# Keeping V of head 0 inside the buffer that the zero fills read, and filling two regions early

## The chip, the cores and the metric

The kernel runs on one core of a Trainium2 chip. The metric is the device time of one execution in microseconds; the kernel before takes 792.94 us (median of three runs, 792.92 to 793.36). Engines are named as the profile names them: PE (matmuls), PEld (its weight loads), DVE, ACT, POOL, and SP, which here only issues transfers and waits. All transfers run on 16 DMA engines, which take work from queues: q1 is filled by SP, q10 by ACT, q0 by POOL.

## What is computed

One decode step of a transformer layer, forward and backward: a layer norm, attention of 16 query heads over 8 cached heads of K and V, a gated feed-forward block, and the gradients of all of it but the second input. Cut to what matters for the transfers:

```python
W = min(4096, max(256, Sk // 4))                  # 4096 of Sk = 32768 rows are attended
k = jnp.repeat(k_cache[:, :, Sk - W:, :], rep, axis=1)
v = jnp.repeat(v_cache[:, :, Sk - W:, :], rep, axis=1)
p = _softmax(jnp.einsum("bhqd,bhkd->bhqk", q, k) * (Dh ** -0.5), axis=-1)
o = jnp.einsum("bhqk,bhkd->bhqd", p, v)
...
_out, _vjp = jax.vjp(_f, A_x, A_k_cache, A_v_cache, A_wq, A_wo, B_w_gate, B_w_up, B_w_down)
```

The gradients of the two caches are outputs of 8 x 32768 x 256 bf16 each (134 MB). Rows 0 to 28671 of every head took no part in the attention, so their gradient is zero: 16 regions (8 heads, K and V) of 14336 KB that are only zeros. The last 4096 rows of every head are the computed gradient, 2048 KB for each of K and V. Of the inputs, 2048 KB of K and of V are read for each head, and the weights.

## The kernel before

**On-chip memory.** A tile `zeros` (128 partitions x 8192 bf16, 16 KB a partition) is cleared at the start, half on DVE (L55) and half on POOL (L56). All else that is large lives in one tile, `arena`, cut by hand into slots of 16 KB a partition: six for V (`VB`, `HELD = 6`), two at `MB`, three and some at `RB`. A slot holds K or V of one head, 32 rows of 256 on each partition.

**Phase 1** (L360 to L371) runs over heads 0 to 7. For head g, `scores` (L300) transposes K on PE, takes dot products and the softmax; `moments` (L333) scales K by the probabilities on DVE (L341), multiplies it with V on PE (L345) and accumulates the weighted sums of V and K (L349). While head g is in `moments`, `scores` of g+1 runs beside it. K and V of the next heads are loaded into slots that come free (`NEXT`, L355), from ACT's queue.

**Phase 2** (L386 to L525) is one row through the output projection, the feed-forward block and back, and waits mostly for weights and short dependent steps.

**Phase 3** (L620 to L690) runs over the heads again, in the order 2 to 7, 0, 1. For each head `dots` (L278) is run on V, the gradient of K and V is made on PE (L659) and cast into two `stage` slots by ACT and DVE (L663 to L667), and ACT's queue writes the two slots out (L669). V of heads 2 to 7 is still in its slots. V of heads 0 and 1 was overwritten in phase 1 by K of heads 3 and 4, and is loaded a second time (`V_again`, L631). Beside it POOL makes the weight gradients as outer products (L551, L580 to L583) and sends them out on its own queue. Slots of V that are done with serve as stages and hold `dg_bc` and the second copy of the first weight (`wq2A`).

**The fills.** SP's instruction stream is in order: the weight, then K and V of the first heads, then from L250 the 16 zero fills, each one transfer that writes a region of 14336 KB as 896 rows of 16 KB out of 32 of the partitions of `zeros`. Two are under way at a time (`DEEP = 2`): a fill is issued when the one two places before it has landed. Region 8 is split (`UNEVEN`, L240 to L246) into two entries of this list: a small one of 2048 KB, which is three transfers (1536, 480 and 32 KB), two of them with an outer dimension of only 3 and 2, and the remaining 12288 KB.

The Python order is not the order on an engine: a scheduler sorts each engine's instructions by its own estimates, and slots are guarded by semaphores that it derives. Only the fills and their waits are kept out of that, in program order.

Of the kernel before, what the change touches and what calls it, by code (L numbers as in the profile page):

```python
# [7 lines left out]
bf16 = mybir.dt.bfloat16  # L8
f32 = mybir.dt.float32
AX = mybir.AxisListType.X  # L10
ALU = mybir.AluOpType
# [4 lines left out]
G = 8  # L16
Dh = 256
W = 4096
T = 32
F = 1792  # L20
FH = F // 2
NB = 7
Sk = 32768
EPS = 1e-5
SCALE = 1.0 / 16.0
ZW = 8192
NZ = (Sk - W) * Dh // (128 * ZW)
ZM = 5120
DEEP = 2
UNEVEN = 8  # L30
HELD = 6
KB = 512


@with_exitstack
def kernel(
        ctx, tc, A_x, A_k_cache, A_v_cache, A_wq, A_wo, B_x, B_w_gate, B_w_up, B_w_down, grad_out,
           out_0, out_1, out_2, out_3, out_4, out_5, out_6, out_7, out_8):
    nc = tc.nc
    LD = nc.scalar  # L40
    ZQ = nc.sync

    const = ctx.enter_context(tc.tile_pool(name="const", bufs=1))
    small = ctx.enter_context(tc.tile_pool(name="small", bufs=2))
# [3 lines left out]


    VB = 0  # L50
    MB = VB + HELD * 16 * KB
    RB = MB + 32 * KB
    TOTAL = RB + 105 * KB // 2
    zeros = const.tile([128, ZW], bf16)
    nc.vector.memset(zeros[:, 0:ZM], 0.0)  # L55
    nc.gpsimd.memset(zeros[:, ZM:ZW], 0.0)  # L56
    arena = const.tile([128, TOTAL], bf16)

    def ar(off, n):
        return arena[:, off:off + n]  # L60

    def kv(off):
        return ar(off, T * Dh).rearrange("p (t d) -> p t d", d=Dh)

    V_of = [kv(VB + 16 * KB * (g % HELD)) for g in range(G)]
    K_of = [kv(o * KB) for o in (RB // KB, RB // KB + 16, MB // KB + 16, 0, 16, RB // KB, RB // KB + 16, RB // KB)]
    M_sb = [ar(MB + 4 * KB * g, 4 * KB).bitcast(f32).rearrange("p (v h d) -> p v h d", v=2, h=2) for g in range(G)]
    wqA = ar(MB, 24 * KB).rearrange("p (c j) -> p c j", c=3)
    wqB = ar(MB + 24 * KB, 4 * KB)
# [21 lines left out]
    h_row = ar(XB + FH + D, 2 * D)[0:1].bitcast(f32)  # L91
    h2_bf = ar(XB + FH, D)[0:1]

    stage = [kv(o) for o in (RB, RB + 16 * KB, VB + 32 * KB, VB + 48 * KB)]
    P3 = RB + 32 * KB
    rTm = [ar(P3 + 2 * i * KB, 2 * KB).rearrange("p (l c) -> p l c", l=8) for i in range(2)]
    R_sb = [ar(P3 + (4 + i) * KB, KB) for i in range(2)]
# [3 lines left out]
    VT_slot = [ar(P3 + 17 * KB // 2 + 2 * i * KB, 2 * KB) for i in range(3)]  # L101
    rows2 = ar(P3 + 29 * KB // 2, 2 * KB)[0:16].bitcast(f32)
    dqrow = [ar(P3 + 33 * KB // 2 + 2 * i * KB, 2 * KB)[0:16].bitcast(f32) for i in range(2)]
    dg_bc = ar(VB + 64 * KB, 2 * F).rearrange("p (i f) -> p i f", i=2)
    dq_bc = ar(MB, H * Dh)
    wst = [ar(MB + (8 + 12 * i) * KB, 12 * KB) for i in range(2)]
    wq2A = ar(VB + 72 * KB, 24 * KB).rearrange("p (c j) -> p c j", c=3)
    wq2B = ar(P3 + 33 * KB // 2, 4 * KB)

    x_bf = const.tile([1, D], bf16)  # L110
# [3 lines left out]
    wq_A = A_wq[0:384, :].rearrange("(p c) j -> p c j", c=3)  # L114
    wq_B = A_wq[384:D, :].rearrange("r (h j) -> (r h) j", h=2)
# [5 lines left out]
    ident_f = const.tile([128, 128], f32)  # L121
# [17 lines left out]
    nc.vector.reduce_sum(out=tl32, in_=ident_f[:].rearrange("p (k i) -> p k i", i=4), axis=AX)  # L139
    tl_f = const.tile([128, 8], f32)  # L140
    nc.vector.reduce_sum(out=tl_f[:], in_=tl32.rearrange("p (q l) -> p l q", q=4), axis=AX)
    half_f = const.tile([128, 4], f32)
    nc.vector.memset(half_f[:, 0:3], 1.0)
    nc.vector.memset(half_f[:, 3:4], 0.5)
# [53 lines left out]
    def load_kv(dst, cache, g, queue=LD):  # L198
        queue.dma_start(out=dst, in_=cache[0, g, Sk - W:, :].rearrange("(p t) d -> p t d", t=T))

    load_kv(K_of[0], A_k_cache, 0, ZQ)
    load_kv(V_of[0], A_v_cache, 0, ZQ)
    load_kv(K_of[1], A_k_cache, 1, ZQ)
    load_kv(V_of[1], A_v_cache, 1, ZQ)
    load_kv(V_of[2], A_v_cache, 2, ZQ)

    rstd1, xnT_f, X1_b = layernorm(x_bf[:], bf16, "ln1")
    d2_ps = ps_t.tile([128, 4], f32, tag="tmp")
# [19 lines left out]
    qT_bf = const.tile([128, 32], bf16)  # L228
    nc.vector.tensor_copy(out=qT_bf[:].rearrange("p (g k e) -> p k e g", k=2, e=2), in_=qT_ps[:])

    load_kv(K_of[2], A_k_cache, 2, ZQ)
    for g in range(3, HELD):
        load_kv(V_of[g], A_v_cache, g, ZQ)

    fills = []
    for g in range(G):
        for o in (out_2, out_3):
            reg = o[0, g, 0:Sk - W, :].rearrange("s d -> (s d)")
            n = NZ
            if len(fills) == UNEVEN:  # L240
                odd = reg[0:128 * ZW].rearrange("(r f) -> r f", f=ZW)
                n = NZ - 1
                reg = reg[128 * ZW:NZ * 128 * ZW]
                fills.append([(odd[0:96].rearrange("r f -> (r f)").rearrange("(p f) -> p f", p=128), zeros[:, 0:ZW * 3 // 4]),
                              (odd[96:126].rearrange("(e n) f -> e n f", e=3), zeros[0:12:4].unsqueeze(1).to_broadcast([3, 10, ZW])),
                              (odd[126:128], zeros[0:8:4])])  # L246
            fills.append([(reg.rearrange("(p n f) -> p n f", p=32, f=ZW), zeros[0:128:4].unsqueeze(1).to_broadcast([32, 4 * n, ZW]))])
    zsem = [tc.alloc_semaphore(f"zsem{j}") for j in range(DEEP)]
    due = [0] * DEEP
    for i, parts in enumerate(fills):  # L250
        j = i % DEEP
        if i >= DEEP:
            tc.keep_in_program_order(ZQ.wait_ge(zsem[j], due[j]))
        for dst, src in parts:
            fill = ZQ.dma_start(out=dst, in_=src)
            tc.info.no_tile_sem_insts.add(fill.ins.name)
            tc.add_to_no_dep_group("fills", fill.ins)
            tc.keep_in_program_order(fill.then_inc(zsem[j], 16))
            due[j] += 16
    for j in range(DEEP):  # L260
        filled = tc.keep_in_program_order(ZQ.wait_ge(zsem[j], due[j]))
    tc.declare_fence(filled.ins, group="fills")

    pT_all = const.tile([128, G, T, 2], bf16)
    oT_f = const.tile([128, 2, H], f32)
# [29 lines left out]
    with tc.tile_pool(name="ps_m", bufs=1, space=bass.MemoryType.PSUM) as ps_m, \  # L295
# [56 lines left out]
            for vh in range(2):  # L352
                nc.scalar.copy(out=M_sb[g][:, vh].rearrange("p h d -> p (h d)"), in_=M_ps[:, vh, :])

        NEXT = {0: ((0, 3), (0, 5)), 1: ((0, 4), (0, 6)), 3: ((1, 6),), 4: ((1, 7),), 5: ((0, 7),)}  # L355
        wo_v = A_wo.rearrange("(p j) n -> p j n", j=32)
        wd_v = B_w_down.rearrange("(h p b) n -> h p b n", h=2, b=NB)
        JW = 19
# [2 lines left out]
        for g in range(G):  # L361
            p_f = p_next
            if g + 1 < G:
                p_next = scores(g + 1)
            moments(g, p_f)
            for w, h in NEXT.get(g, ()):
                load_kv((K_of, V_of)[w][h], (A_k_cache, A_v_cache)[w], h)
            if g == G - 2:
                LD.dma_start(out=wo_sb[:, JW:], in_=wo_v[:, JW:])
                LD.dma_start(out=wd_sb, in_=wd_v[0])  # L370
# [15 lines left out]
    with tc.tile_pool(name="ps_mid", bufs=3, space=bass.MemoryType.PSUM) as ps_mid, \  # L386
# [38 lines left out]
        for h in range(2):  # L425
# [3 lines left out]
            for c in range(2):  # L429
                cs = slice(c * D, (c + 1) * D)  # L430
                for i in range(2):
                    r = 2 * c + i
# [46 lines left out]
        for jc in range(32):  # L479
# [3 lines left out]
                                in1=m8_f[:].unsqueeze(2).to_broadcast([128, 8, 32]), op=ALU.mult)  # L483
# [43 lines left out]
    with tc.tile_pool(name="work2", bufs=2) as work2, tc.tile_pool(name="lnw", bufs=1) as lnw, \  # L527
# [86 lines left out]
        plan = [[dq_all], [job_d(0), job_d(1)], [job_o(0, 13), job_o(13, 13)], [job_o(26, 6), spread_all, job_g(0)], [job_g(1), job_gB()],  # L614
                [job_q(0), job_q(1)], [job_q(2), job_qB()], []]

        order = list(range(2, G)) + [0, 1]
        V_again = [kv(VB), kv(VB + 16 * KB)]
        stc = 0
        for it, g in enumerate(order):  # L620
            V_sb = V_of[g] if it < HELD else V_again[g]
            fill_vpad(it % 2, doT_bf[:, :, 2 * g:2 * g + 2])

            def evac(q, XT, ps):
# [2 lines left out]
                else:  # L627
                    nc.vector.tensor_copy(out=XT, in_=ps)
            dpT_ps = dots(V_sb, VT_slot, vpad[it % 2], rows2, ps_t, "tmp", evac)
            if it in (4, 5):  # L630
                load_kv(V_again[it - 4], A_v_cache, it - 4)  # L631
            if it == 3:
                for c in range(3):
                    LD.dma_start(out=wq2A[:, c, :], in_=wq_A[:, c, :])
                LD.dma_start(out=wq2B, in_=wq_B)

            pds = work2.tile([128, 4, 8, 4], bf16, tag="pds")
            pv = pT_all[:, g].rearrange("p (q l) h -> p q l h", q=4)
# [10 lines left out]
            R_ps = ps_t.tile([128, 2, 2, 128], f32, tag="tmp")  # L649
            nc.tensor.matmul(R_ps[:].rearrange("p w e n -> p (w e n)"), lhsT=se, rhs=Zrow, start=True, stop=True)  # L650
            nc.scalar.copy(out=Rs.rearrange("p (w n e) -> p w e n", w=2, e=2), in_=R_ps[:])
            stV, stK = stage[stc % 4], stage[(stc + 1) % 4]
            stc += 2
            for l in range(8):
                for qp in range(2):
# [11 lines left out]
                        nc.vector.tensor_copy(out=stK[:, t:t + 2, :], in_=d_ps[:, :, 1, :])  # L667
            for o_ap, st_ in ((out_3, stV), (out_2, stK)):
                LD.dma_start(out=o_ap[0, g, Sk - W:, :].rearrange("(p t) d -> p t d", t=T), in_=st_)  # L669
            for job in plan[it]:  # L670
                job()
            if it == HELD:
                dn1 = lnw.tile([128, 5], f32)
                for c in range(3):
                    nc.vector.tensor_tensor_reduce(out=wq2A[:, c, :], in0=wq2A[:, c, :], in1=dq_bc, scale=1.0, scalar=0.0,
                                                   op0=ALU.mult, op1=ALU.add, accum_out=dn1[:, c:c + 1])
                for h in range(2):
                    nc.vector.tensor_tensor_reduce(out=wq2A[:, h, 0:HJ], in0=wq2B, in1=dq_bc[:, h * HJ:(h + 1) * HJ], scale=1.0, scalar=0.0,
                                                   op0=ALU.mult, op1=ALU.add, accum_out=dn1[:, 3 + h:4 + h])
                dcat1 = lnw.tile([128, 8], f32)  # L680
                close(dn1, dcat1)
                dxT = layernorm_bwd(dcat1, xnT_f, rstd1, dhT[:], "ln1")
                dx_ps = ps_t.tile([1, D], f32, tag="tmp")
                for c in range(3):
                    nc.tensor.matmul(dx_ps[0:1, c * 128:(c + 1) * 128], lhsT=dxT[:, c:c + 1], rhs=ident_f[:], start=True, stop=True)
                nc.tensor.matmul(dx_ps[0:1, 384:D], lhsT=dxT[:, 3:4], rhs=pair_f[:], start=True, stop=True)
                dx_bf = x_bf
                nc.vector.tensor_copy(out=dx_bf[:, 0:384].rearrange("o (p c) -> o p c", c=3), in_=dx_ps[0:1, 0:384].rearrange("o (c p) -> o p c", c=3))
                nc.vector.tensor_copy(out=dx_bf[:, 384:D], in_=dx_ps[0:1, 384:D])
                LD.dma_start(out=out_1.rearrange("a b d -> (a b) d"), in_=dx_bf[:])  # L690
# [29 lines left out]
```

## Time and profile before

| | |
|---|---|
| median of three runs | 792.94 us (792.92 to 793.36) |
| the profiled execution | 794.59 us, of which the span from first to last instruction is 792.8 us |
| DMA | 334.58 MB in 24109 packets, mean 422 GB/s; 53.58 MB read from HBM, 280.59 MB written |
| busy in the span | PE 60%, DVE 45%, ACT 25%, PEld 25%, POOL 22% |
| fills on SP's queue | 15 of 14336 KB (median 87.6 us from issue to landing), 12288, 1536, 480 and 32 KB |
| V loads | 6 from SP's queue (median 28.3 us to landing), 4 from ACT's (16.9 us), 2048 KB each |
| last instruction on POOL | issue of the last weight gradient, 732.41 us |

Times in the trace are microseconds from the start of the span. A stretch's row in the windows view has the busy time of each engine, then the granted share of the PE clock, then the share of the 16 DMA engines that was busy, and the GB/s that they moved.

### The profile page before, as it was taken

How to read it: one execution, taken by the hardware profiler on the slowest of the kernel's cores; microseconds unless marked ns; L12 is line 12 of the kernel's file. 1: busy time of each engine (PE TensorE's matmuls, PEld its weight loads, DVE VectorE, ACT ScalarE, POOL GpSimd, SP SyncE). 2: the span in 40 equal slices, each digit the busy share in tenths (PEclk: the TensorE clock that was granted, in tenths of full speed). 3: DMA queues.
4: the chain of work that ended last, by engine and by line, in shares of the span. 5: the costliest groups of instructions: out<-in, count | busy, mean ns of one | idle time of the engine just before them, and what ended most of it. 6: DMA issues, size and time to landing. Idle time of an engine off the chain costs nothing.

```text
span 792.8 us, 6367 instructions
## 1 busy us (share of the span) xinstructions
PE 476.8 (60%) x2165; PEld 201.4 (25%) x2184; DVE 358.5 (45%) x1083; ACT 198.2 (25%) x309; POOL 176.2 (22%) x93
## 2 busy tenths in 40 slices
PE   4899999999969935222325898618478273430000
PEld 1444444444424422000112433203123121000000
DVE  4266263736533631043785732965585184540000
ACT  0621325241304000010101633424244153440000
POOL 1000000000000000000000029869051865658000
PEclk9889999999998976555555999657578575555555
DMA  9999999999999999999899999999999999999997
GB/s 378 427 420 433 425 429 431 429 427 428 430 426 432 425 428 430 430 429 431 381 427 433 422 424 418 430 425 425 430 416 430 426 428 432 427 424 428 427 428 308
DMA packets 24109, 334.58 MB, mean 422 GB/s; under 512 B 1289, under 2 KB 2317, under 8 KB 3693
## 3 DMA queue, kind: packets, MB, share of 16 engines
q1 hardware_dynamic: 16229, 257.43, 76.5%
q10 hardware_dynamic: 5560, 60.23, 17.9%
q0 software_dynamic: 2288, 16.52, 5.0%
q8 instruction: 17, 0.28, 0.1%
q14 instruction: 15, 0.12, 0.0%
HBM read 53.58 MB, written 280.59 MB: 421 GB/s over the span
## 4 chain that ended last, share of the span: by engine, by line
PE 37%; DMA 20%; POOL 17%; DVE 8%; issue 6%; another core or an unknown queue 2%; ACT 1%; POOLq 0%; SPq 0%; ACTq 0%; DVEq 0%
POOL arena L551 14%; DMA out_dram<-arena 11%; PE M_ps L345 11%; PE rows_ps L288 6%; PE ok_ps L349 6%; PE tr_ps L285 6%; DVE arena L480 2%; DMA arena<-in_A_wo_dram 2%; DVE arena L341 2%; DMA arena<-in_A_k_cache_dram 2%; DMA arena<-in_B_w_down_dram 2%; DMA arena<-in_B_w_up_dram 2%; DVE arena L423 2%; DMA arena<-in_A_wq_dram 1%
## 5 line engine op out<-in xcount | busy, mean ns | idle before, releaser
L341 DVE TENSOR_SCALAR arena<-arena,p_f 128x256 bf16<-128x256 bf16 x512 | 109.0, 280 | 56.7 <-PE M_ps L345 28.0
L345 PE MATMUL M_ps<-arena 128*128 128x512 bf16 x493 | 118.9, 382 | 0.6
L285 PE MATMUL tr_ps<-ident_f,arena 128*128 128x128 f32 x512 | 96.5, 318 | 35.9 <-DMA arena<-in_A_v_cache_dram 15.6
L288 PE MATMUL rows_ps<-arena,vpad 128*16 128x512 bf16 x256 | 89.5, 445 | 8.5 <-ACT arena L626 3.1
L659 PE MATMUL d_ps<-arena 32*128 32x512 bf16 x256 | 48.6, 507 | 75.4 <-DVE arena L667 65.5
L302 ACT COPY arena<-tr_ps 128x1024 bf16<-128x1024 bf16 x64 | 63.7, 1013 | 119.6 <-PE tr_ps L285 117.8
L285 PEld LDWEIGHTS tr_ps<-ident_f,arena 128*128 128x128 f32 x512 | 63.2, 158 | 88.9 <-issue 33.7
L551 POOL TENSOR_SCALAR arena<-arena,xT 128x1792 bf16<-128x1792 bf16 (+1 forms) x9 | 60.5, 6734 | 61.2 <-DMA out_dram<-arena 33.8
L663 ACT CAST arena<-d_ps 128x512 bf16<-128x512 f32 x64 | 38.0, 593 | 103.2 <-PE d_ps L659 94.9
L373 POOL DMA_DIRECT2D arena<-in_A_wo_dram x1 | 0.7, 687 | 278.6 <-PE ok_ps L349 278.6
L345 PEld LDWEIGHTS <-arena 128*128 128x128 bf16 x512 | 48.1, 99 | 56.0 <-issue 7.7
L666 DVE CAST arena<-d_ps 128x512 bf16<-128x512 f32 x64 | 44.0, 687 | 40.4 <-PE d_ps L659 40.1
L551 POOL TENSOR_SCALAR arena<-dh_bc,oX_f 128x448 bf16<-128x448 bf16 x32 | 52.9, 1665 | 9.9 <-DMA out_dram<-arena 9.7
L349 PE MATMUL ok_ps<-arena 128*32 128x512 bf16 x256 | 52.5, 381 | 1.4 <-DVE arena L329 0.9
L667 DVE CAST arena<-d_ps 128x512 bf16<-128x512 f32 x64 | 43.5, 679 | 14.5 <-DMA out_dram<-arena 14.5
L626 ACT COPY arena<-tr_ps 128x1024 bf16<-128x1024 bf16 x32 | 32.7, 1026 | 64.8 <-PE rows_ps L288 36.5
L664 ACT CAST arena<-d_ps 128x512 bf16<-128x512 f32 x64 | 38.4, 600 | 13.5 <-DMA out_dram<-arena 13.5
L659 PEld LDWEIGHTS <-arena 32*128 32x128 bf16 x256 | 10.9, 95 | 110.1 <-DVE arena L667 72.2
L434 PE MATMUL r_ps<-arena,X2pad 128*4 128x448 bf16 x24 | 10.4, 571 | 38.8 <-DMA arena<-in_B_w_up_dram 23.7
L288 PEld LDWEIGHTS <-vpad 128*16 128x16 bf16 x256 | 17.0, 91 | 46.8 <-issue 42.0
L551 POOL TENSOR_SCALAR arena<-dh_bc,hh_f 128x448 bf16<-128x448 bf16 x14 | 19.4, 1398 | 42.8 <-PE dqb_ps L533 42.8
L384 ACT CAST arena<-bc_ps 128x448 bf16<-128x448 f32 x16 | 8.7, 541 | 80.8 <-PE bc_ps L383 69.7
(218 smaller groups left out, 429.4 us busy)
## 6 DMA issues: line engine op xcount, KB each, us to landing
out_dram<-zeros SPq DMA_DIRECT2D x15, 14336.0 KB, 87.6
out_dram<-arena ACTq DMA_DIRECT2D x16, 2048.0 KB, 29.0
arena<-in_A_v_cache_dram SPq DMA_DIRECT2D x6, 2048.0 KB, 28.3
out_dram<-zeros SPq DMA_DIRECT2D x1, 12288.0 KB, 33.7
arena<-in_A_k_cache_dram ACTq DMA_DIRECT2D x5, 2048.0 KB, 14.8
arena<-in_A_v_cache_dram ACTq DMA_DIRECT2D x4, 2048.0 KB, 16.9
arena<-in_A_k_cache_dram SPq DMA_DIRECT2D x3, 2048.0 KB, 21.0
arena<-in_A_wq_dram SPq DMA_DIRECT2D x1, 3072.0 KB, 10.1
```

The costliest lines, as they stand in the source:

```text
L285: nc.tensor.transpose(tr_ps[:, i, :], X_sb[:, 4 * q + i, :].bitcast(f32), ident_f[:])
L288: nc.tensor.matmul(rows_ps[:], lhsT=pad[:, e, 16 * q:16 * q + 16], rhs=XT.rearrange("p (n e) -> p n e", e=2)[:, :, e], start=(q == 0 and e ...
L302: sT_ps = dots(K_of[g], KT_slot, vpad[g % 2], rows1, ps_c, "cols", lambda q, XT, ps: nc.scalar.copy(out=XT, in_=ps))
L341: nc.vector.tensor_scalar(out=pK[:, i, hh, :], in0=K_sb[:, t, :], scalar1=p_f[:, 8 * i + c, hh:hh + 1], scalar2=None, op0=ALU.mult)
L345: nc.tensor.matmul(M_ps[:, vh, :], lhsT=V_sb[:, t, vh * 128:(vh + 1) * 128], rhs=pK[:, i, :, :].rearrange("p h d -> p (h d)"), start=(t == ...
L349: nc.tensor.matmul(ok_ps[32 * k:32 * (k + 1), :], lhsT=ppad[g % 2][:, t:t + 2, :].rearrange("p t h -> p (t h)"), rhs=X_sb[:, t:t + 2, :].r ...
L551: nc.gpsimd.tensor_scalar(out=buf[:, off:off + n], in0=src, scalar1=col, scalar2=None, op0=ALU.mult)
L659: nc.tensor.matmul(d_ps[:, qi].rearrange("p w d -> p (w d)"), lhsT=rm[32 * q:32 * (q + 1), l, :], rhs=Rs[32 * q:32 * (q + 1), :], start=Tr ...
L663: nc.scalar.copy(out=stV[:, t:t + 2, :], in_=d_ps[:, :, 0, :])
L664: nc.scalar.copy(out=stK[:, t:t + 2, :], in_=d_ps[:, :, 1, :])
L666: nc.vector.tensor_copy(out=stV[:, t:t + 2, :], in_=d_ps[:, :, 0, :])
L667: nc.vector.tensor_copy(out=stK[:, t:t + 2, :], in_=d_ps[:, :, 1, :])
```

## The change

The tile `zeros` is gone, and V gets a seventh slot. V of head 0 stays in slot `S[0]` for the whole kernel. Once head 0 is through `moments`, `clear_rows` (DVE) clears every fourth partition of that slot, 32 of the 128, by an AND of 32-bit words with a mask of -1 or 0 per partition. The fills from region 2 on read these 32 partitions; the other 96 keep V.

Regions 0 and 1 are filled before that, from slots 5 and 6, which POOL clears at the start (128 x 16384). These two early fills write 448 rows of 32 KB each. V of heads 5 and 6 is loaded into the slots from POOL's queue behind a wait for the early fills.

In phase 3 the order of the heads is 3, 1, 4, 5, 0, 6, 2, 7. After head 3 its slot takes a copy of slot 0 (DVE), and a load of 32 partitions puts the missing quarter of V of head 0 into that copy. V of head 2, whose slot was taken by K of head 6 and V of head 7, is loaded again into the same slot after head 0. V of head 1 is now kept. The split region 8 is one entry of the list: its four transfers are issued together on one semaphore. Stages, `dg_bc` and `wq2A` move to other slots, and `wq2A` is loaded in two parts.

```diff
+ZE = 32 * KB
+ZW = 16 * KB
+EARLY = 2
-    zeros = const.tile([128, ZW], bf16)
-    nc.vector.memset(zeros[:, 0:ZM], 0.0)
-    nc.gpsimd.memset(zeros[:, ZM:ZW], 0.0)
...
-    K_of = [kv(o * KB) for o in (RB // KB, RB // KB + 16, MB // KB + 16, 0, 16, RB // KB, RB // KB + 16, RB // KB)]
+    S = [VB + 16 * KB * i for i in range(7)]
+    V_of = [kv(S[i]) for i in (0, 1, 2, 3, 4, 5, 6, 2)]
+    K_of = [kv(o) for o in (RB, RB + 16 * KB, S[4], MB + 16 * KB, RB, RB + 16 * KB, S[2], RB)]
+    Z_early = ar(S[5], ZE)
+    Z_late = ar(S[0], ZW)
+    nc.gpsimd.memset(Z_early, 0.0)
...
+    keep_f = small.tile([128, 1], f32, tag="keep", bufs=1)
+    nc.vector.reduce_sum(out=keep_f[:], in_=ident_f[:, 0:128:4], axis=AX)
+    nc.vector.tensor_scalar(out=keep_f[:], in0=keep_f[:], scalar1=-1.0, scalar2=None, op0=ALU.add)
+    keep_i = const.tile([128, 1], mybir.dt.int32)
+    nc.vector.tensor_copy(out=keep_i[:], in_=keep_f[:])
...
+    for reg in regions[:EARLY]:
+        fill_with(reg.rearrange("(p n f) -> p n f", p=32, f=ZE), rows_of(Z_early, NZ * ZW // ZE), esem, "early")
+    early = tc.keep_in_program_order(nc.gpsimd.wait_ge(esem, 16 * EARLY))
+    tc.declare_fence(early.ins, group="early")
+    for g in (5, 6):
+        load_kv(V_of[g], A_v_cache, g, nc.gpsimd)
...
+    def fill_late():
+        zsem = [tc.alloc_semaphore(f"zsem{j}") for j in range(DEEP)]
+        due = [0] * DEEP
+        for i, reg in enumerate(regions[EARLY:]):
+            j = i % DEEP
+            if i >= DEEP:
+                tc.keep_in_program_order(ZQ.wait_ge(zsem[j], due[j]))
...
+            for dst, src in parts + [(reg.rearrange("(p n f) -> p n f", p=32, f=ZW), rows_of(Z_late, n))]:
+                fill_with(dst, src, zsem[j], "fills")
+                due[j] += 16
...
+    def clear_rows():
+        words = Z_late.bitcast(mybir.dt.int32)
+        nc.vector.tensor_tensor(out=words, in0=words, in1=keep_i[:].to_broadcast([128, ZW // 2]), op=ALU.bitwise_and)
...
-        NEXT = {0: ((0, 3), (0, 5)), 1: ((0, 4), (0, 6)), 3: ((1, 6),), 4: ((1, 7),), 5: ((0, 7),)}
+        NEXT = {0: ((0, 4),), 1: ((0, 5),), 2: ((1, 4), (0, 6)), 4: ((0, 7),), 6: ((1, 7),)}
...
+            if g == 1:
+                clear_rows()
+                fill_late()
             moments(g, p_f)
...
-        order = list(range(2, G)) + [0, 1]
-        V_again = [kv(VB), kv(VB + 16 * KB)]
-        for it, g in enumerate(order):
-            V_sb = V_of[g] if it < HELD else V_again[g]
+        for it, g in enumerate((3, 1, 4, 5, 0, 6, 2, 7)):
+            V_sb = kv(S[3]) if g in (0, 2) else V_of[g]
...
-            if it in (4, 5):
-                load_kv(V_again[it - 4], A_v_cache, it - 4)
...
+            if it == 0:
+                nc.vector.tensor_copy(out=ar(S[3], 16 * KB), in_=Z_late)
+                LD.dma_start(out=ar(S[3], 16 * KB)[0:128:4], in_=A_v_cache[0, 0, Sk - W:, :].rearrange("(p t) d -> p (t d)", t=T)[0:128:4])
+            if it == 3:
+                LD.dma_start(out=wq2A[:, 0, :], in_=wq_A[:, 0, :])
+                LD.dma_start(out=wq2B, in_=wq_B)
+            if it == 4:
+                load_kv(kv(S[3]), A_v_cache, 2)
+            if it == 5:
+                for c in range(1, 3):
+                    LD.dma_start(out=wq2A[:, c, :], in_=wq_A[:, c, :])
```

## The prediction

> **What bounds the kernel now.** I read the page's slices and queues first:
>
> ```profile
> span 792.8 us, 6367 instructions
> ...
> DMA  9999999999999999999899999999999999999997
> GB/s 378 427 420 433 425 429 431 429 427 428 430 426 432 425 428 430 430 429 431 381 427 433 422 424 418 430 425 425 430 416 430 426 428 432 427 424 428 427 428 308
> ...
> q1 hardware_dynamic: 16229, 257.43, 76.5%
> q10 hardware_dynamic: 5560, 60.23, 17.9%
> q0 software_dynamic: 2288, 16.52, 5.0%
> ...
> HBM read 53.58 MB, written 280.59 MB: 421 GB/s over the span
> ```
>
> The DMA engines are 90% busy or more in all slices but two, while no compute engine is over 60%. Bytes bound this kernel. Besides the first slice (378 GB/s, transfers are starting), two moved less: the one around 386 us (381) and the last (308). The queue rows price a byte: q1 used 0.765 x 792.8 us of all 16 engines for 257.43 MB, 2.36 us a MB; q10, which has loads and computed outputs, 0.179 x 792.8 / 60.23 = 2.36 too. So direction and queue do not matter, only the sum.
>
> Then what SP, which issues the fills, waited for:
>
> ```profile
> SPq L255 <- DMA out_dram<-zeros: 637.3, 15, 66.0
> SPq L261 <- DMA out_dram<-zeros: 95.2, 1, 95.2
> ```
>
> It only ever waits for its own fills, and its last wait is 95.2 us long. So is the end fill, or compute? The stretches after POOL's last instruction say:
>
> ```profile
> 732.41 0.62 POOL L606 DMA_DIRECT2D out_dram<-arena  x1 [0.30 <-POOL arena L583]
> ```
>
> ```profile
> 744.00:748.00 4.00, 0.00 (x0) 0.00 (x0) 0.00 (x0) 0.00 (x0) 0.00 (x0) 0.50 1.00 420
> 748.00:752.00 4.00, 0.00 (x0) 0.00 (x0) 0.00 (x0) 0.00 (x0) 0.00 (x0) 0.50 1.02 434
> ...
> 784.00:788.00 4.00, 0.00 (x0) 0.00 (x0) 0.00 (x0) 0.00 (x0) 0.00 (x0) 0.50 0.75 319
> 788.00:792.00 4.00, 0.00 (x0) 0.00 (x0) 0.00 (x0) 0.00 (x0) 0.00 (x0) 0.50 0.07 29
> ```
>
> Until 748 some of the traffic is computed output (the packet records of q0 and q10 end there). From 748 on the engines are full with fills alone, some 37 us of them, and then run out unevenly: by 788 to 792 only 7% of them still work. Compute may therefore end up to about 37 us later at no cost, and a byte that is not moved shortens the end.
>
> The weak slice, closer:
>
> ```profile
> 384.00:386.00 2.00, 0.68 (x2) 0.00 (x0) 1.82 (x4) 0.53 (x1) 0.00 (x0) 0.50 0.99 422
> 386.00:388.00 2.00, 0.00 (x0) 0.00 (x0) 2.00 (x5) 0.00 (x0) 0.00 (x0) 0.50 0.65 277
> 388.00:390.00 2.00, 0.47 (x1) 0.10 (x1) 2.00 (x7) 0.53 (x1) 0.00 (x0) 0.50 0.39 168
> 390.00:392.00 2.00, 0.09 (x1) 0.00 (x0) 1.68 (x4) 0.53 (x1) 0.00 (x0) 0.50 0.93 391
> ```
>
> Lost here: 2 x (0.35 + 0.61 + 0.07) = 2.06 us of all engines. At that time the second place of the two fills was held by the small 2048 KB entry of the split region, so engines that were done with region 7 and their part of it had nothing queued until SP saw region 7 land.
>
> **The change part by part.**
>
> *Loads of V.* Before there are 10 of 2048 KB (8 and two again). After: 8, head 2 again, and a quarter (512 KB) for head 0, so 9.25. That takes away 0.75 x 2.097 = 1.573 MB. The regions written are the same. At 2.36 us a MB: -3.7 us, all of it on the bound.
>
> A rule speaks against the full price. The Trainium skill, "DMA: Bandwidth & Descriptors", section "Rules for kernel authors", wants 128 partitions and at least 1 MiB per transfer for full bandwidth; this load has 32 and half of that. With the fit that this page gives in its section "Anatomy of one DMA — SWDGE (gpsimd) path" (2.0 us plus bytes over 436 GB/s) as an estimate, the quarter would cost 3.2 us instead of 1.2, the saving be 1.7 and the time near 789.7. The trace says otherwise so far: the fills read just 32 partitions at 434 GB/s (748 to 752), and a load's fixed time is covered when other work is queued; but no run shows a 512 KB load alone on its queue.
>
> *Larger rows.* The two early fills have 448 rows of 32 KB instead of 896 of 16 KB. The packet records cost 309 ns at 8 KB, 611 at 16 KB and 912 at 24 KB, so about 9 ns a packet are overhead: 56 fewer packets on each of 16 engines save 0.5 us. The 32 KB size itself is not in the trace: from 0 to -0.5, I take -0.3.
>
> *The split region as one entry.* Its four transfers are issued together, so 12288 KB stand behind the small parts and the engines do not run dry in mid-run: at most -2.1 us. But the end is set by the slowest engine, not by the mean. Sorted into 16 back-to-back chains, the packet records show 11 chains idle there for about 1 to 4 us and 5 not at all, and at the end chains that stop between 785.9 and 790.9. If the last one is one of the five, nothing is won. From 0 to -2.1; I take -1.2, between, as 11 of 16 idled but the next chain ends only 1.6 us before the last.
>
> *The start.* Clearing slots 5 and 6 on POOL costs by this row's rate (2.66 us for 3072 columns) 14.2 us instead of 2.7, and the identity matrices are made behind it on POOL:
>
> ```profile
> 0.73 2.66 POOL L56 MEMSET zeros<- 128x3072 bf16 x1 [0.29 <-POOLq L704]
> ...
> 3.96 0.29 POOL masks.py:199 TENSOR_SCALAR_AFFINE_SELECT ident_f<-ident_f 128x128 f32<-128x128 f32 x1
> ```
>
> So `ident_f` comes at about 15.8 instead of 4.25, the DVE reductions of it follow (with three short ones for the mask), and the first q matmul, which waited for its weight until 12.08, waits until about 20.8: +8.7 us for compute. SP issues seven loads (18.4 MB, 43 us of traffic) before it needs q, so its next load and the early fills come at about 30 us, with the queue still full. Cost 0; without that cover, 1 us per us.
>
> *Clearing 32 rows.* One DVE operation on 4096 words of 32 bits, two inputs. Nearest rows:
>
> ```profile
> L675 DVE CUSTOM_DVE_ANT_0 arena<-arena 128x4096 bf16<-128x4096 bf16 x3 | 13.3, 4433 | 22.0 <-DMA arena<-in_A_wq_dram 22.0
> ...
> L55 DVE MEMSET zeros<- 128x2560 uint32 x1 | 2.2, 2192 | 1.3 <-PEq L704 1.3
> ```
>
> Between 3.5 us (4096 words at the memset's 0.86 ns) and 4.4 us (4096 elements, two inputs); I take 4.4. It stands on DVE behind 16 products of head 1 and must wait until PE has read V of head 0 for the last time (63 to 67 us before, about 75 now). In the trace DVE idles 5.3 us at that place anyway. The late fills wait for it on SP, nothing else does: they are issued at about 85, while loads and early fills (18.4 + 2.1 + 29.4 MB) last to about 118. Cost 0.
>
> *V of heads 5 and 6 from POOL's queue.* They start when the early fills have landed, about 120 to 128, and share the engines with late fills: landed by about 150. `moments` of head 5 needs them at about 200. POOL has nothing else to do (its first wait before is 278.6 us long). Cost 0.
>
> *K and V late in phase 1.* K of head 7 comes a head earlier, V of head 7 a head later, after `moments` of head 6. Gone is PE's wait for K:
>
> ```profile
> 238.23 1.97 PE L285 MATMUL tr_ps<-ident_f,arena 128*128 128x128 f32 x8 [7.09 <-DMA arena<-in_A_k_cache_dram]
> ```
>
> In its place `moments` of head 7 waits for V for the landing time, 15.5 to 20 us: compute +8 to +13.
>
> *Phase 3.* DVE copies a slot (8192 bf16): 3.5 us at the memset's rate, 8.9 at that of L675; I take 5.5 (L628's 686 ns per 1024). ACT's queue then holds the quarter load ahead of head 3's casts, so they wait for the copy: +5.5. The second iteration stages into the slot from which the first one's V gradient is still being sent (29.0 us median to landing, from 458.6): 0 to 8 more. POOL's chain only follows by what comes before it.
>
> *Sum for compute*: 8.7 + 0 to 4.4 + 8 to 13 + 3.5 to 8.9 + 0 to 8 = 20 to 43, likely 27. Its last output, at 748 before, lands at about 775, ahead of the end of the fills at about 786. Cost 0.
>
> *Sum for the end*: -3.7 - 0.3 - 1.2 = -5.2 us. The profiled execution took 794.59 us, 1.79 more than its span, and would take 789.4, its span 787.6. The median of the runs lies 1.65 below that execution: 792.94 - 5.2 = 787.7.
>
> **The rivals.**
>
> 1. *Compute ends last (slower).* Place: POOL's chain of outer products, or the last stages. From a shift of 38 us on, each us costs one; the bounds above reach 43, which gives a span of 791 and no gain; at 47 and more it is slower, and stalls that add up to 50 would give 800. For it: every one of the terms is a wait in series. Against: 27 is likely, and waits for landings shrink when the fills are done early.
>
> 2. *The queue runs dry before the late fills (slower).* If clearing came after about 118 us, DMA would idle by the difference; at 125 the gain is gone, at 127 it is slower. Against: 85 is estimated, and the nearest gap in compute would have to be 33 us.
>
> 3. *Balance eats the gain (same, or barely faster).* The engine that ends last neither idled in mid-run nor gets the full saving, by the short load or by records of instruction fetches that fall on it: about -1.7 to -2.5, 790.4 to 791.3.
>
> 4. *More than the sum.* The mid-run loss is won whole and the ends draw together: -3.7 - 0.5 - 2.1 and 1.5 of the uneven end, 785.1.
>
> **How the numbers follow.** The forecast has 0.75, rival 1 0.10 (of it 0.06 slower, 0.03 same, 0.01 faster), rival 2 0.04, rival 3 0.08, rival 4 0.03. A difference of 0.2% (1.6 us) is about what the measurement can tell. Faster: the forecast, rival 4, most of rival 3: 0.83. Same: 0.07. Slower: 0.10. The range goes from rival 4's 785.1 (785.0) to 791.2, the upper end of rival 3; what lies outside is rival 1's and 2's slower part and a little below.
>
> **What would show it.** Right: HBM read 52.0 MB instead of 53.58; full slices around 386 us; first q matmul near 21 us; SP's waits only for fills, and none before 118 us that leaves DMA idle; last compute output landing near 775, followed by 10 us or so of fills alone; span near 787.6. Wrong: a slice under 9 between 100 and 140 us (rival 2); traffic of q0 or q10 in the last microseconds (rival 1); last chains more than 5 us apart (rival 3).

## The result, and the profile after

| | before | after |
|---|---|---|
| median | 792.97 us (792.92 to 793.36, 4 runs) | 1191.79 us (1191.07 to 1192.34, 4 runs) |
| ratio | | 1.503, 95% interval 1.500 to 1.505 |
| span of the profiled execution | 792.8 us | 1190.1 us |
| granted PE clock, mean | 0.754 | 0.668 |

The change makes the kernel 399 us slower; the prediction was 787.7 us. The time is half as long again. The page of the kernel after, its slices of 29.8 us first:

```profile
span 1190.1 us, 6364 instructions
...
PE   4400897000000000000000499997643379877852
...
DMA  9999329999999999999999230122220031666457
GB/s 395 431 432 416 143 98 415 432 432 431 430 425 431 424 430 425 427 427 428 426 427 428 115 142 1 71 78 96 110 74 0 0 133 72 254 285 258 175 246 330
...
HBM read 52.00 MB, written 280.59 MB: 279 GB/s over the span
```

The bytes are as forecast: 52.00 MB read instead of 53.58, the same written. But PE and the DMA engines, which worked side by side before, now take turns. Where PE is 0, DMA is 9; where PE works, DMA is below 9 in all slices but three (the first, the second and the seventh). There are two long stretches without computing, and after each a stretch in which the DMA engines have little to do. Closer, in stretches of 20 us (busy time of each engine, granted clock, DMA share, GB/s):

```profile
40.00:60.00 20.00, 3.91 (x23) 2.27 (x22) 0.18 (x1) 3.72 (x4) 0.00 (x0) 0.71 1.01 427
60.00:80.00 20.00, 0.00 (x0) 0.00 (x0) 0.00 (x0) 0.00 (x0) 0.00 (x0) 0.50 1.02 441
...
140.00:160.00 20.00, 19.89 (x98) 9.14 (x99) 17.38 (x69) 3.00 (x4) 0.00 (x0) 1.00 0.29 104
...
220.00:240.00 20.00, 0.00 (x0) 0.00 (x0) 0.00 (x0) 0.00 (x0) 0.00 (x0) 0.50 1.00 430
...
640.00:660.00 20.00, 0.00 (x0) 0.00 (x0) 0.00 (x0) 0.00 (x0) 0.00 (x0) 0.50 1.02 433
...
700.00:720.00 20.00, 19.66 (x100) 8.79 (x100) 9.49 (x45) 7.60 (x12) 0.00 (x0) 1.00 0.00 1
```

The view of waits names who stands still and for whom:

```profile
POOL arena L398 <- PE ok_ps L371: 715.4, 1, 715.4
...
PE cols_ps L315 <- DVE arena L312: 545.3, 4, 466.8
DVE arena L312 <- SPq L279: 469.1, 1, 469.1
ACT arena L375 <- SPq L279: 466.8, 1, 466.8
...
DVE arena L293 <- POOLq L253: 79.1, 1, 79.1
```

```profile
SPq L244 <- DVE arena L351: 141.1, 1, 141.1
SPq L279 <- DMA out_dram<-arena: 68.1, 1, 68.1
```

L279 is SP's last wait for the late fills, L253 POOL's wait for the early ones. In the kernel before, the wait that answers to L279 (its L261) has nobody behind it: no row of its view of waits names SP's sequencer as a releaser. Now DVE waits 79.1 us for L253 before it clears a small pad (L293), and 469.1 us for L279 before it copies a row of scores out of PSUM (L312); PE waits for that row. Neither instruction touches slot 0, 5 or 6. DVE's list around the two stops:

```profile
120.74 0.55 DVE L293 MEMSET arena<- 128x256 uint32 x2 [79.08 <-POOLq L253]
```

```profile
668.56 0.68 DVE L312 COPY arena<-rows_ps 16x512 f32<-16x512 f32 x1 [469.14 <-SPq L279]
```

How 1190 comes about: the last computed output had landed at 748 us before and lands at 1188 now. The two stops are 79.1 + 469.1 = 548 us; without them computing takes 640, 108 less than before, most likely because it now runs beside idle queues: a 2048 KB store from ACT's queue lands after 10.6 us (median) instead of 29.0, and the waits of POOL, DVE and ACT for the landing of stores add up to 18.3 us instead of 92.4. All fills are out at about 668 us, and the remaining 520 us belong to computing alone.

Why these instructions wait is in the list of waits of the built program. After:

```
DVE  41   L293 Memset arena 128x256          [waits Pool_sequencer]
DVE  187  L312 TensorCopy arena<-rows_ps     [waits SP_sequencer]
ACT  15   L375 TensorCopy arena<-M_ps        [waits DMA, Pool_sequencer, PE]
ACT  28   L375 TensorCopy arena<-M_ps        [waits SP_sequencer]
POOL 14   L398 DMACopy arena<-in_A_wo_dram   [waits ..., SP_sequencer, ...]
```

In the list of before, the same clearing (L271) and copies (L290) wait for PE or for nothing. `declare_fence` makes the last wait stand for all fills: whoever must come after a fill waits for that wait. A fill reads its source, so a later write into the source must come after it. Before, the source was `zeros`, into which nobody writes later. After, the source is a part of `arena`, into which everybody writes, and many of these writes were ordered behind the fills although they go to other columns. It works the other way too: the clearing of slot 0 is over at 155.1 us (150.71 and 4.42), but the late fills are issued at 175.61, right after the pad copy L351 has ended (175.36 and 0.19), the write that the row of SPq L244 names. That it is such an order is the theory to be tested (theory F, a false order through the shared tile). The rivals are the changes that the prediction had thought of: the clearing that the late fills wait for, loads behind the early fills, the moved copies of V.

### The profile page after: what moved, and what is told of

Read it like the earlier page. It is cut to its first block, busy times and chain, and to the rows that moved or that the text cites. A ratio compares the mean times of both kernels' runs of the same rounds, so it can differ in the third digit from the quotient of the medians.

```text
span 1190.1 us, 6364 instructions
## 1 busy us (share of the span) xinstructions
PE 481.4 (40%) x2165; PEld 203.5 (17%) x2184; DVE 376.4 (32%) x1087; ACT 197.7 (17%) x309; POOL 189.3 (16%) x95
## 4 chain that ended last, share of the span: by engine, by line
another core or an unknown queue 37%; PE 24%; DVE 8%; DMA 6%; POOL 5%; issue 3%; ACT 1%; SPq 1%; POOLq 0%; DVEq 0%; ACTq 0%
PE M_ps L367 7%; DMA out_dram<-arena 5%; PE rows_ps L310 4%; PE tr_ps L307 4%; POOL arena L576 3%; PE ok_ps L371 3%; DVE arena L505 2%; PE d_ps L676 1%; PE dqb_ps L558 1%; DVE arena L448 1%; SPq L244 1%; DVE arena L684 1%; DMA arena<-in_A_wo_dram 1%; DVE arena L651 1%
## 5 line engine op out<-in xcount | busy, mean ns | idle before, releaser
L315 PE MATMUL cols_ps<-ident_f,arena 16*128 16x16 f32 x64 | 7.3, 225 | 545.6 <-DVE arena L312 545.3
L312 DVE COPY arena<-rows_ps 16x512 f32<-16x512 f32 x16 | 10.8, 673 | 473.1 <-SPq L279 469.1
L367 PE MATMUL M_ps<-arena 128*128 128x512 bf16 x493 | 122.2, 390 | 8.2 <-DMA arena<-in_A_v_cache_dram 7.1
L315 PEld LDWEIGHTS cols_ps<-ident_f,arena 16*128 16x128 f32 x64 | 6.0, 154 | 550.4 <-DVE arena L312 549.3
L375 ACT COPY arena<-M_ps 128x512 f32<-128x512 f32 x16 | 8.6, 589 | 540.5 <-SPq L279 466.8
L576 POOL TENSOR_SCALAR arena<-dh_bc,oX_f 128x448 bf16<-128x448 bf16 x32 | 50.2, 1580 | 0.2
L371 PEld LDWEIGHTS <-arena 128*32 128x32 bf16 x256 | 21.7, 97 | 29.2 <-issue 3.6
## 6 DMA issues: line engine op xcount, KB each, us to landing
out_dram<-arena ACTq DMA_DIRECT2D x16, 2048.0 KB, 10.6
```

Of the source, the lines that this page charges most:

```text
L367: nc.tensor.matmul(M_ps[:, vh, :], lhsT=V_sb[:, t, vh * 128:(vh + 1) * 128], rhs=pK[:, i, :, :].rearrange("p h d -> p (h d)"), start=(t == ...
L371: nc.tensor.matmul(ok_ps[32 * k:32 * (k + 1), :], lhsT=ppad[g % 2][:, t:t + 2, :].rearrange("p t h -> p (t h)"), rhs=X_sb[:, t:t + 2, :].r ...
L576: nc.gpsimd.tensor_scalar(out=buf[:, off:off + n], in0=src, scalar1=col, scalar2=None, op0=ALU.mult)
```

## The experiments

**1. The two slots as tiles of their own.** Nothing else is edited: the instructions, the transfers and their bytes are the same. Only the scheduler, which now sees three tiles, sorts a part of the instructions of DVE, ACT and PE otherwise.

```diff
-    arena = const.tile([128, TOTAL], bf16)
+    arena = const.tile([128, TOTAL - 48 * KB], bf16)
+    late_t = const.tile([128, 16 * KB], bf16)
+    early_t = const.tile([128, 32 * KB], bf16)
     def ar(off, n):
+        if off < 16 * KB:
+            return late_t[:, off:off + n]
+        if 80 * KB <= off < 112 * KB:
+            return early_t[:, off - 80 * KB:off - 80 * KB + n]
+        off -= 16 * KB + 32 * KB * (off >= 112 * KB)
```

> The changed kernel with slot 0 and slots 5 and 6 as tiles of their own beside the arena; the same slots, transfers and operations. Theory F (false waits): the two stops of compute in the changed kernel (43 to 122 us, and 203 to 664 us) come from writes to other parts of the same tile that were ordered behind the last wait of the fills; with own tiles both stops are gone, and the first forecast's sum holds: -3.7 -0.3 -1.2, so 785 to 791 us, full DMA slices from 20 to 780 us. Theory R (real waits): the stops come from what the change truly makes wait (POOL's long clearing, the slots of heads 5 and 6, the late V loads); then they stay, above 1100 us.

Measured: 789.86 us (789.71 to 790.41); ratio to the kernel before, beside which it ran (793.07), 0.9957, interval 0.9940 to 0.9973. All 402 us are gone, and the kernel is faster than the one before. Its page:

```profile
span 788.1 us, 6396 instructions
...
PE   1999999999689939234042248997536506535120
...
DMA  9999999999999999999999999999999999999996
...
HBM read 52.00 MB, written 280.59 MB: 422 GB/s over the span
```

No row of its waits has SP's sequencer as the releaser, and DMA is full in every slice but the last, at 386 us too. This shows theory F as a whole; what it doesn't yet show is which of the two tiles does what, and whether V has anything to do with it.

**2 and 3. One slot of the two at a time.** In the first only `late_t` is a tile of its own, in the second only `early_t`.

> Only slot 0 (source of the 14 late fills) is a tile of its own; slots 5 and 6 stay in the arena. Theory F: the second stop (461 us) goes, the first (79 us, until the early fills have landed) stays; the last computed output, at 748 us before, shifts by about 27 + 79 us to some 850, the fills are done before that, so 840 to 870 us with a DMA share under 1 at the end. Theory R: no change against the changed kernel (1190), or both stops gone (785 to 791).

> Only slots 5 and 6 (source of the two early fills) are a tile of their own; slot 0 stays in the arena. Theory F: the first stop goes, the second stays until the last late fill has landed. All fills and the loads up to there, about 262 MB at 2.36 us a MB, end near 620 us instead of 664; the rest took 526 us after the stop in the changed kernel, so 1130 to 1165 us. Theory R: 1190 as before, or 790.

Measured, one run each: 821.13 us with only the late slot apart, 1144.84 us with only the early ones apart. The waits of the first, then of the second:

```profile
DVE arena L296 <- POOLq L256: 81.2, 1, 81.2
```

```profile
DVE arena L316 <- SPq L283: 505.9, 1, 505.9
...
ACT arena L379 <- SPq L283: 503.5, 1, 503.5
```

Each tile has its own stop, and taking it out of the shared tile takes that stop away and leaves the other. The second came out as expected. The first was expected 20 to 50 us later than it came; where its 31 us over experiment 1 are spent is plain. The first stop delays the clearing of slot 0 (DVE, 150.96 us instead of 69.38), so the late fills are issued at 155.41 us, while the early ones had landed by about 121, and between the two the queues hold a few loads only:

```profile
120.00:140.00 20.00, 16.74 (x77) 7.43 (x78) 12.14 (x57) 7.54 (x14) 1.23 (x2) 0.83 0.53 210
140.00:160.00 20.00, 20.00 (x101) 9.11 (x99) 17.37 (x70) 3.00 (x4) 0.00 (x0) 1.00 0.29 89
160.00:180.00 20.00, 20.00 (x100) 8.30 (x99) 11.02 (x54) 7.79 (x12) 0.00 (x0) 1.00 0.99 420
```

Of the stretch from 120 to 160 about 24 us are lost (20 x 0.47 + 20 x 0.71). The rest goes at the end, where the fills are out at 790 us and SP waits for the last store of the computation:

```profile
SPq L746 <- DMA out_dram<-arena: 26.9, 1, 26.9
```

So here the prediction's rivals 1 and 2 both come true, but as consequences of a stop of 81 us that neither of them contains.

**4. One tile, other partitions.** If the order is false, it must hang on how the fills' reads are described. Here everything stays in `arena`, but slot 0 is cleared in partitions 0 to 31 and the fills read these, so that no read has a step between its partitions (V of head 0 gets its missing quarter there too).

```diff
-        return src[0:128:4].unsqueeze(1).to_broadcast([32, n, src.shape[1]])
+        return src[0:32].unsqueeze(1).to_broadcast([32, n, src.shape[1]])
```

> One arena as in the changed kernel, but the fills read partitions 0 to 31 instead of every fourth one, and the same 32 partitions are cleared and reloaded. The program's list then has no wait of DVE or ACT on the fills' last wait left in phase 1. Theory F in its narrow form (it is the step of four partitions in the fills' access pattern that made other writes to the tile look as if they overlapped): both stops go although all is still one tile; if the fills keep their rate, 785 to 791 us. Theory R: both stops stay, above 1100 with compute idle from 43 to 122 us. The Trainium skill, "SBUF — State Buffer", section "Door 1: The DMA port swizzle", has partitions 0 to 31 on half of the ports, at half the rate: by that page the 268 MB of fill would move at about 218 GB/s, and as an estimate the time would be 1250 to 1450 us, with compute running on through it.

Measured: 1326.63 us (one run), for another reason. The stops are gone: no engine waits for SP's last wait, computing is spread over the first 29 slices, and the longest wait is POOL's own for the early fills, behind which its loads of V stand:

```profile
POOL arena L205 <- POOLq L253: 181.7, 1, 181.7
```

So the false order needs both, the shared tile and the step of 4 partitions. What in the derivation of the order takes such a read for one that overlaps was not looked into. But the fills now crawl:

```profile
DMA  9999999999999999999999999999999999999995
GB/s 399 345 243 282 272 255 334 254 233 300 245 256 226 231 244 206 206 244 276 296 250 285 312 274 262 214 280 288 276 272 224 206 205 205 205 206 205 206 205 129
```

The engines count as full, yet where fills are alone they move 205 to 206 GB/s, against 434 before; the median packet of 16 KB takes 1226 ns instead of 611. The Trainium skill, "SBUF — State Buffer", section "Door 1: The DMA port swizzle", has this: what counts for a transfer is how many of 16 ports its partitions reach, and partitions 0 to 31 reach 8. The trace agrees: 205 GB/s are 0.47 of 434. So of these two sources only the one with the step of 4 gives the fills their rate, and it is this step with which the order comes out false. (The 268 MB of the expectation are both gradients whole; the zero fills are 234.9 MB of them. With that, at the 218 GB/s of the expectation and 2.36 us for each of the other 98 MB, the estimate is about 1310 us, inside the same range.)

**5. The cause alone, in the kernel before.** No V moves, no fill changes, no wait is added: `zeros` is only made a part of the large tile, in columns that nobody else writes.

```diff
-    zeros = const.tile([128, ZW], bf16)
+    arena = const.tile([128, TOTAL + ZW], bf16)
+    zeros = arena[:, TOTAL:TOTAL + ZW]
     nc.vector.memset(zeros[:, 0:ZM], 0.0)
     nc.gpsimd.memset(zeros[:, ZM:ZW], 0.0)
-    arena = const.tile([128, TOTAL], bf16)
```

> Only one thing is done to the kernel before: its zero buffer becomes the last 8192 columns of the large tile; nobody but the two clearing instructions writes there, no V moves, no fill changes its size or its place in the queue. If it is enough that the fills read, with a step of 4 partitions, a tile that the computation writes, then everything the program orders behind the last fill's completion stands still: from about 25 to 32 us until all 234.9 MB of fills and the loads ahead of them are out, (234.9 + 22.6) MB x 2.36 us = 608 us, and then the rest of the computation runs over almost idle DMA queues. In the changed kernel computing took 1184.9 - 79.1 - 461 = about 645 us without its two stops, of which about 30 would be done here before the stop: 608 + 615 = about 1220 us, range 1170 to 1260. If the stops came from the moves of V, from the clearing or from the loads behind the early fills, this kernel has none of them and takes 793 us.

Measured: 1202.49 us (one run). One stop, over at 609.62 us where 608 was worked out from the bytes:

```profile
609.62 0.55 DVE L271 MEMSET arena<- 128x256 uint32 x2 [577.21 <-SPq L261]
```

The rivals that need V, the clearing or the moved loads are out: none of these is in this kernel, and it is as slow as the changed one.

**6. The split region as one entry, alone.** What is left is the forecast's own sum, which experiment 1 missed by 2 us (787.7 against 789.86). This run prices one of its terms in the kernel before.

```diff
-            fills.append([... three small parts ...])
-            fills.append([... 12288 KB ...])
+            fills.append([... three small parts ..., ... 12288 KB ...])
```

> The kernel before with one thing changed: the split region's four transfers are one entry of the list of fills, on one semaphore. This prices the term taken at -1.2 us (bounds 0 and -2.1). If a stretch in which the queue runs partly empty costs the end what it loses: 791.0 to 792.2 us, and the dip at 384 to 392 us is gone. If the end is set by something that the dip doesn't move: 793.0 +- 0.4.

Measured: 792.80 us (11 runs) beside 793.11 for before (21 runs); ratio 0.9994, interval 0.9986 to 1.0003. The dip is gone, and nothing is won that could be told from zero:

```profile
384.00:388.00 4.00, 0.39 (x1) 0.00 (x0) 4.00 (x9) 0.00 (x0) 0.00 (x0) 0.50 0.99 423
388.00:392.00 4.00, 0.55 (x1) 0.10 (x1) 3.67 (x10) 1.06 (x2) 0.00 (x0) 0.50 1.04 443
...
782.00:786.00 4.00, 0.00 (x0) 0.00 (x0) 0.00 (x0) 0.00 (x0) 0.00 (x0) 0.50 0.41 176
786.00:790.00 4.00, 0.00 (x0) 0.00 (x0) 0.00 (x0) 0.00 (x0) 0.00 (x0) 0.50 0.12 53
```

Before, the last stretches were 0.98 (782 to 786) and 0.33 (786 to 790). The packet records, sorted into 16 chains, end between 780.7 and 788.9 us (mean 784.3) instead of between 785.9 and 790.9 (mean 787.4). Part of that shift is the execution: the profiled one of before took 794.59 us, this one 792.67. The spread, 8.2 us instead of 5.0, is seen in one execution of each; in the three other traces with the split region as one entry and without stops it is 8.3 to 9.8 us. The mean chain ends earlier, the last one hardly.

**7. The bytes.** Experiment 1, but V of head 0 is loaded whole a second time, as before the change.

```diff
-                nc.vector.tensor_copy(out=ar(S[3], 16 * KB), in_=Z_late)
-                LD.dma_start(out=ar(S[3], 16 * KB)[0:128:4], in_=A_v_cache[0, 0, Sk - W:, :]...[0:128:4])
+                load_kv(kv(S[3]), A_v_cache, 0)
```

> The kernel with the two slots as tiles of their own (789.86 us), but V of head 0 is loaded whole again (2.097 MB) instead of being copied on DVE with a quarter (0.524 MB) loaded: 1.573 MB more. If the bytes set the end: +3.7 us, 793.0 to 794.0 us. If the last stores of the computation set it, the bytes cost only what they delay those: 789.5 to 791.5 us, and the copy that goes from DVE gives a little back.

Measured: 793.52 us (793.21 to 794.90, 11 runs; before 793.11): 3.66 us more than experiment 1, which was timed beside 793.07 for before. The fastest run here is 2.8 us above the slowest of experiment 1. The bytes cost what the forecast took for them, 3.7 us, although without DVE's copy the last stores of the computation are issued 13 us earlier (744.0 instead of 757.1 us).

**8. Computing earlier.** Experiment 1, but the identity matrices are made ahead of the clearing, and DVE does 20 of its 32 KB a partition.

```diff
-    nc.gpsimd.memset(Z_early, 0.0)
     make_identity(nc, ident_f[:])
+    nc.vector.memset(Z_early[:, 0:20 * KB], 0.0)
+    nc.gpsimd.memset(Z_early[:, 20 * KB:ZE], 0.0)
```

> The kernel with the two slots as tiles of their own, but the identity is made ahead of the clearing of slots 5 and 6, and DVE and POOL share that clearing (20 and 12 of 32 KB of a row). Computing should start some 7 to 9 us earlier (the q row at 22 to 24 us instead of 30.88). If the last two stores of the computation (issued at 757 us, landed at about 785) hold up the end, they land at about 777 to 780 and the end falls to 786.5 to 788.5 us. If the bytes and the uneven ends of the 16 engines set it, nothing moves: 789.4 to 790.3 us. If compute's start is swallowed on the way by waits for landings, the last stores are issued within 2 us of before and nothing is told of the end.

Measured: 789.66 us (789.51 to 791.74, 5 runs); ratio 0.9959, interval 0.9946 to 0.9971. Computing starts 9.2 us earlier (the q row is copied at 21.71 us instead of 30.88), and its last output is issued at 743.58 instead of 757.56 us. In experiment 1 the last microseconds belong to such stores: from 772 to 780 us the traffic is 0.67 of q10 and 0.25 of fills. Here q10 is empty from 764 us on, and 0.92 are fills. And the end stays where it was, as the last stretches show, first of experiment 1, then of this one:

```profile
776.00:780.00 4.00, 0.00 (x0) 0.00 (x0) 0.00 (x0) 0.00 (x0) 0.00 (x0) 0.50 0.80 340
780.00:784.00 4.00, 0.00 (x0) 0.00 (x0) 0.00 (x0) 0.00 (x0) 0.00 (x0) 0.50 0.33 139
784.00:788.00 4.00, 0.00 (x0) 0.00 (x0) 0.00 (x0) 0.00 (x0) 0.00 (x0) 0.50 0.05 20
```

```profile
776.00:780.00 4.00, 0.00 (x0) 0.00 (x0) 0.00 (x0) 0.00 (x0) 0.00 (x0) 0.50 0.79 336
780.00:784.00 4.00, 0.00 (x0) 0.00 (x0) 0.00 (x0) 0.00 (x0) 0.00 (x0) 0.50 0.29 123
784.00:788.00 4.00, 0.00 (x0) 0.00 (x0) 0.00 (x0) 0.00 (x0) 0.00 (x0) 0.50 0.04 16
```

The last stores of the computation fill the end only as long as they are there; when they are gone, fills take their place. With experiment 7 this shows that the bytes set the time, and that computing, at 757 us, is still inside its slack. That the uneven end of the 16 engines takes what is left is what the chains suggest; no run tests it. The chains of packets end between 777.7 and 786.0 us in experiment 1 (mean 780.6), between 776.9 and 785.7 here (mean 780.7), between 781.0 and 790.8 in experiment 7 (mean 784.5).

Experiments 1 and 8 are faster than both kernels, by 0.4% against the one before. The second, at 789.66 us, differs from the first by less than the runs can tell. Experiment 7, also with the slots apart but without the saved bytes, is as slow as before.

## Why the prediction was wrong

**The step that failed** is under *Clearing 32 rows*: "The late fills wait for it on SP, nothing else does [...] Cost 0." It looked at what the fills wait for, and never at who waits for the fills. Before, that question had the answer "nobody", and the text used it: SP's last wait of 95.2 us was taken as a sign that fills end the kernel, which is right, and, without a word, as harmless for the rest, which was right only while the fills read a tile that nobody wrote. The change moves their source into the tile in which all computing is done. The same gap stands under *V of heads 5 and 6 from POOL's queue*, also with "Cost 0": POOL's wait for the early fills held DVE for 79.1 us, SP's wait for the late ones held it for 469.1. Experiment 5 does nothing but move the source and costs 409 us; experiment 1 undoes that alone and gives 402 back.

**The rivals.** None of the four holds this. Rival 1 (compute ends last, from a shift of 38 us on) and rival 2 (the queue runs dry, once the late fills come after 118 us) name the right places and were bounded by sums of small waits, 43 us and 33 us. In the changed kernel the late fills come at 175.6 and computing ends 440 us later, both for one reason that has no term in the sum. The range had no room for it, and the 0.10 for slower was given to other mechanisms.

**The terms of the sum**, as experiment 1 and its variations measure them, where the stops are absent:

| term | forecast | measured |
|---|---|---|
| loads of V, 1.573 MB less | -3.7 | -3.66 (experiment 7 against 1) |
| split region as one entry | -1.2 (0 to -2.1) | -0.3, not told from 0 (experiment 6) |
| rows of 32 KB | -0.3 (0 to -0.5) | not timed alone; a packet takes 1213 ns (median) against 2 x 611, 0.5 us for each engine |
| clearing 32 rows | 4.4 on DVE | 4.42 |
| copy of a slot on DVE | 5.5 (3.5 to 8.9) | 2.29, below the lower bound |
| the start | +8.7 on computing | q row at 30.88 instead of 21.50: +9.4 |
| computing in all | last output at 748 lands at 775 (20 to 43 later) | issued at 757, lands at about 785: +37 |
| the end | -5.2 | -3.2 (interval -4.8 to -2.1) |

So the sum for the end was too large by 2.0 us, of which experiment 6 finds some 0.9 in the split region. The prediction had said of this term that the end is set by the slowest engine, and that 5 of 16 chains did not idle in mid-run: "If the last one is one of the five, nothing is won." It then took the middle. The run shows the other case: the mean of the chains comes earlier, and the spread grows from 5.0 to 8.2 us. That is rival 3 (balance eats the gain, 790.4 to 791.3), half a microsecond better than it was priced, and its sign, last chains more than 5 us apart, came too (8.3 us in experiment 1). Where the remaining 1.1 us went is within the interval of experiment 1 and stays open.

**The rule weighed against the trace.** The Trainium skill, "DMA: Bandwidth & Descriptors", section "Rules for kernel authors", wants 128 partitions and at least 1 MiB per transfer; by the fit that the prediction takes from the same page, an estimate, the quarter load would have cost so much that the saving was 1.7 us. Experiment 7 measures 3.66: a load of 512 KB into 32 partitions, with other work queued on the engines, costs its bytes, and no more than that can be seen. The time of experiment 1 happens to lie near the 789.7 worked out from that rule, but the term that it concerns came out by the trace's price.

**What was right**: bytes bound the kernel (experiment 7), computing had slack for the 37 us by which it came later (experiment 8: taking 14 us of them back makes no difference), and 52.00 MB read. These could only show once the false order was gone.

## What to carry to other kernels

When a buffer that transfers read or write moves into a tile that others use, ask who will be ordered behind those transfers, by the derived waits and not by the data: a fence that stands for many transfers is free while nobody waits for it, and costs their whole duration when somebody does. Read the waits of the built program, on every engine, as well as the order of its instructions; here one line of that list (DVE, L312, waits for SP) stands for 469 of the 548 us of stops. Where a buffer must be read with a step between partitions, give it a tile of its own, even if its bytes are reused for something else.

## What the runs showed of the hardware

- A stop of computing does not leave the time untouched on the other side: with idle queues a 2048 KB store lands in 10.6 us (median) instead of 29.0, and the whole computation, without its stops, takes 640 us instead of 748. In experiment 5, where computing is that of the kernel before, it takes 622 (the last output lands at 1198.8, the stop is 577.2). How the 108 and 126 us divide between landings of loads and of stores was not measured.
- Reading 32 neighbouring partitions instead of 32 with a step of 4 halves the rate of a fill, 205 against 434 GB/s, while the engines still count as fully busy (experiment 4). Busy time alone doesn't tell a slow transfer from a full one; the GB/s beside it does.
- While POOL clears 128 x 16384 (0.72 to 14.47 us), a DVE copy of a single row, 0.20 us before the change, is held until that is over, and the next instruction with it:

```profile
0.72 13.75 POOL L74 MEMSET early_t<- 128x16384 bf16 x1 [0.29 <-POOLq L739]
```

```profile
2.59 11.96 DVE L170 COPY dup_t<-x_bf 1x128 bf16<-1x128 bf16 x1
2.71 11.84 DVE L180 BATCH_NORM_AGGREGATE mv<-stats 1x2 f32<-1x6 f32 x1
```

  Both lists are of experiment 1; the changed kernel shows the same (11.97 and 11.85 us). DVE's own clearings beside it, from 0.82 to 2.2 us (0.06 to 0.55 us each), were not held. In experiment 8, where the copy comes after POOL is done, it takes 0.21 us. The Trainium skill, "SBUF — State Buffer", section "SBUF: two separate sides", states that DVE and POOL share one pair of ports, which a DVE operation needs in a two-port mode or with two inputs, and that whichever starts first holds it for the whole instruction while the other blocks; these rows agree, if the copy runs in such a mode, which the trace does not say. No cost shows here, since DVE next needed the identity matrix that POOL made behind the clearing.
